# Reading the moving operand of the three-pass products in pairs of columns, and putting the columns back on the way out of PSUM

## The chip, the cores and the metric

The kernel runs on one core of one Trainium2 chip. The metric is the device time of one execution in microseconds (us); for the kernel before, three runs gave a median of 481.45 us, from 481.04 to 482.91 us.

## What is computed

The reference is a linear-attention recurrence whose output, laid out by token, goes through a two-matrix feed-forward block with a smooth gate:

```
for t in range(S):                                  # S = 768, batch 4, 8 heads, head size 48
    cur = einsum('bhd,bhe->bhde', u * k[t], v[t])
    y[:, :, t] = einsum('bhd,bhde->bhe', r[t], state + cur)
    state = w * state + einsum('bhd,bhe->bhde', k[t], v[t])
x = y as 3072 tokens x 384
h = x @ w_in                                        # 384 x 2048
g = h * tanh(softplus(h))
out = g @ w_out                                     # 2048 x 384
```

All inputs and the output are float32.

## The kernel before

**Groups and tiles.** The 768 time steps are cut into 6 groups (`NC`) of 128 steps; a group has 4 attention steps (one per batch row, `B`), and so 512 tokens (`T`). For each group the feed-forward block runs over 16 tiles of 128 hidden features (`NF`), two of which make a batch (`FB`). An up tile multiplies 3 slices of `w_in` (`KT`) with the group's x into one PSUM bank `hp` of 128 x 512; there are two such banks, used in turn. A copy, on VectorE (DVE) or ScalarE (ACT), takes `hp` to `hb` in SBUF (`evacuate`, L1214). ACT then runs Sigmoid, Arctan and Sin over the batch of two tiles (L1025 to L1031), DVE multiplies (L1041), and the result is split into a high part `gh` (L1045) and a rest `gl` (L1049). A down tile multiplies `gh` and `gl` with slices of `w_out` and adds into three PSUM banks `acc0` to `acc2`, which stay open over all 16 tiles of a group; then `put` (L1069) copies them out and sends them to memory.

**Three-pass products.** From the second group on, every product is made of three matmuls in the type float32r (four bytes an element): high weight by high operand, high weight by rest, rest of the weight by high operand. In `matmul(out, lhsT, rhs)` the `lhsT` is the stationary operand (the weights, 128 x 128) and `rhs` the moving one (128 x 512):

```
for n, (a, m) in enumerate(((wh, mh), (wh, ml), (wl, mh))):
    matmul(out, lhsT=a, rhs=m, start=first and n == 0, stop=last and n == 2, skip_group_check=skip)
```

`up` (L1013) calls it for `hp`, with x read as four runs of 128 elements, 256 apart; `down` (L1053) calls it for `acc`, with 512 elements in a row; so does `down_last` (L1320) for the last batch, written out by pass. In the first group, the up tiles 8 to 15 (`FROM`) are three-pass products on `xp` (`up_unit`, L1098), with 512 elements in a row; the down tiles 14 and 15 (`FROM2`) are three-pass products in `down_unit` (L1131). All other products of the first group are plain float32 ones, which the machine runs as two passes each, on weights left in their raw words (`wraw`, every second 32-bit word of the raw block is used). The trace names float32r as f32.

**Order.** The program is written out in full, with an order per engine that a planner works out (`Flow`): each piece of work names what it waits for and its cost on an engine, and the planner runs a list schedule. `tile_cost` (L1078) gives the costs of up and down tiles, `dve` and `act` those of the copies. The order of TensorE is mostly: up tiles of the next batch, down tiles of an earlier one, with the attention steps between. Loads go out on SP, stores mostly on ACT's queue. `matmul` at L355 is the helper that issues every matmul, so all of TensorE has this one line and the tiles tell them apart.

Of the kernel before, what the change touches and what calls it, by code (L numbers as in the profile page):

```python
# [28 lines left out]
KT = DM // 128  # L29
NF = DFF // 128  # L30
# [21 lines left out]
T = B * C  # L52
# [17 lines left out]
UNITS = [(h, c) for h in range(2) for c in range(AHEAD)] + [(None, f) for f in range(WG * AHEAD, NF)]  # L70
# [24 lines left out]
FROM, FROM2 = 8, 14  # L95
# [129 lines left out]
def dve(cols, fast=False):  # L225
    return {"dve": 0.06 + cols / (1900 if fast else 950)}


def act(cols):
    return {"act": 0.1 + cols / 1060}  # L230


class Us(float):
    n = 0
# [10 lines left out]
def pe(us, n):  # L245
    us = Us(us)
    us.n = n
    return {"pe": us}
# [3 lines left out]
def rwkv_mish_kernel(ctx, tc, rkT, rkN, vN, wT, w_in, w_out, consts, rkF, vF, wF, uF, outT):  # L252
    nc = tc.nc
# [99 lines left out]
    def matmul(out, lhsT, rhs, **flags):  # L353
        nonlocal count
        ins = nc.tensor.matmul(out, lhsT=lhsT, rhs=rhs, **flags)  # L355
        first, count = count, count + (4 if lhsT.dtype == F32 else 2)
        k = (count - 1 - BLOCK0 % BLOCK) // BLOCK
        if k != (first - 1 - BLOCK0 % BLOCK) // BLOCK:
            crossed[k] = ins
        return ins  # L360
# [95 lines left out]
    def convert(c):  # L456


        v = nc.vector
        yield f"raw{c}"  # L460
        yield f"issued{c}"
        if c >= 2:
            yield f"whole{c - 2}"
        raw = raws[c]
        up, low = raw[:, :, 1], raw[:, :, 0]
        r = low.bitcast(F32)
        yield act(WE)
        nc.scalar.activation(r, low, AF.Copy, bias=2.0, scale=2.0**-51)
        yield dve(WE, True)
        e = stage.tile([128, WE], F32, name="we", tag="we", bufs=2)  # L470
        eu = e.bitcast(U32)
        v.tensor_scalar(out=eu, in0=up, scalar1=3, scalar2=None, op0=ALU.logical_shift_left)
        yield dve(WE)
        v.scalar_tensor_tensor(out=eu, in0=up, scalar=0x80000000, in1=eu, op0=ALU.bitwise_and, op1=ALU.bitwise_xor)
        yield dve(WE)
        v.tensor_tensor(out=up.bitcast(I32), in0=e.bitcast(I32), in1=r.bitcast(I32), op=ALU.add)  # L476
        whole[W_ORDER[c]] = up.bitcast(F32)
        flow.set(f"whole{c}")
        flow.set("e%d,%d" % W_ORDER[c])
# [501 lines left out]
    def hp_tile(event=None):  # L981
        hp_log.append(event)
        return halves[len(hp_log) % 2]
# [12 lines left out]
    def three(out, wh, wl, mh, ml, first, last, skip=False):  # L996
        for n, (a, m) in enumerate(((wh, mh), (wh, ml), (wl, mh))):
            matmul(out, lhsT=a, rhs=m, start=first and n == 0, stop=last and n == 2, skip_group_check=skip)
# [14 lines left out]
    def up(o, j, event=None):  # L1013
        f, T = o.f + j, o.T
        hp = hp_tile(event)
        for k in range(KT):
            fs = slice((k * WG + f % WG) * 128, (k * WG + f % WG + 1) * 128)
            w = parts[0, f // WG]
            three(hp[:, :T], w[:, 0, fs], w[:, 1, fs], o.x[:, k, :, 0], o.x[:, k, :, 1], k == 0, k == KT - 1)
        return hp[:, :T]  # L1020


# [27 lines left out]

    accs = {}

    def down(o, j):  # L1053
        f = o.f + j
        for mt in range(KT):
            if f == 0:
                accs[mt] = ps.tile([128, 512], F32, name=f"acc{mt}", tag=f"acc{mt}")
            ws = slice(f % WG * DM + mt * 128, f % WG * DM + (mt + 1) * 128)
            a = accs[mt][:, : o.T]
            w = parts[1, f // WG]  # L1060
            three(a, w[:, 0, ws], w[:, 1, ws], o.gh[:, j], o.gl[:, j], f == 0, f == NF - 1)

    def out_buffer(mt):

        if mt < 2:
            return stage.tile([128, 512], F32, name="ob", tag="ob")
        return stage.tile([128, WE], F32, name="we", tag="we", bufs=2)

    def put(engine, mt, T, *cols, queue=nc.scalar):  # L1069
        ob = out_buffer(mt)  # L1070
        (nc.scalar.copy if engine == "act" else nc.vector.tensor_copy)(out=ob[:, :T], in_=accs[mt][:, :T])  # L1071
        n = T // len(cols)
        for k, at in enumerate(cols):
            queue.dma_start(outT[mt * 128 : (mt + 1) * 128, at], ob[:, k * n : (k + 1) * n])
# [23 lines left out]
    def up_unit(n):  # L1098
        h, c = UNITS[n]
        if n >= BY_STEP:  # L1100
            flow.fill = None
        hp = hp_tile(f"h{n}")
        if n < BY_STEP:
            return hp
        if h is None and c >= FROM:
            w, xp = parts[0, c // WG], x_parts[0]
            for k in range(KT):
                fs = slice((k * WG + c % WG) * 128, (k * WG + c % WG + 1) * 128)
                three(hp, w[:, 0, fs], w[:, 1, fs], xp[:, 0, k], xp[:, 1, k], k == 0, k == KT - 1)
            return hp  # L1110
        for i in range(1 if h is None else WG):
            f = c if h is None else c * WG + i
            at, steps = (slice(0, T), slice(0, B)) if h is None else (slice(i * HT, (i + 1) * HT), slice(2 * h, 2 * h + 2))
            for k in range(KT):
                fs = slice((k * WG + f % WG) * 128, (k * WG + f % WG + 1) * 128)
                matmul(
                    hp[:, at], lhsT=whole[0, f // WG][:, fs], rhs=xs[0][:, k, steps, 0], start=k == 0, stop=k == KT - 1
                )
        return hp
# [93 lines left out]

    def evacuate(n, o, j, h):  # L1214
        engine = yield {**dve(o.T), **act(o.T)}
        (nc.scalar.copy if engine == "act" else nc.vector.tensor_copy)(out=o.hb[:, j], in_=h)  # L1216
        flow.set(f"h{n}")

    def second(b):
# [100 lines left out]
    def down_last(b):  # L1320

        o, w = batches[b], parts[1, NW - 1]
        n = FB * b + o.n - 1

        def products(mt, j, low):
            f = o.f + j
            ws = slice(f % WG * DM + mt * 128, f % WG * DM + (mt + 1) * 128)
            for k in range(1 if low else 2):
                matmul(
                    accs[mt][:, :T], lhsT=w[:, k, ws], rhs=(o.gl if low else o.gh)[:, j], start=False,  # L1330
                    stop=low and f == NF - 1,
                )

        yield "w1,%d" % (NW - 1)
        for j in range(o.n):
            yield f"high{b},{j}"
            yield pe(0.92, 8)
            for mt in range(2):
                products(mt, j, False)
        yield f"gated{b}"  # L1340
        for mt in range(KT):
            yield pe(0.46 if mt < 2 else 1.4, 4 if mt < 2 else 12)
            for low in (True,) if mt < 2 else (False, True):
                for j in range(o.n):
                    products(mt, j, low)
            flow.start(output(NC - 1, mt), n - L_PUT)

    def output(g, mt):
        engine = yield {**dve(T), **act(T)} if g < NC - 1 else act(T)
        last = g == NC - 1 and mt < KT - 1  # L1350
        put(engine, mt, T, slice(g * T, g * T + T), queue=nc.sync if last else nc.scalar)
        flow.set(f"put{g},{mt}")


# [32 lines left out]
    for c in range(len(W_ORDER)):  # L1387
        i, f = W_ORDER[c]
# [16 lines left out]
    with tc.If(in_range < 128 * N_FLAGS):  # L1405
# [48 lines left out]
        with tc.tile_pool(name="any2", bufs=1) as work:  # L1454
            raws = [work.tile([128, WE, 2], U32, name=f"raw{i}") for i in range(2)]
            ws = [work.tile([128, 2, WE], F32R, name=f"ws{i}") for i in range(2)]
# [8 lines left out]
            o = Batch()  # L1465
# [5 lines left out]
            with tc.For_i(0, S, 128) as t0:  # L1471
                for b in range(B):
# [4 lines left out]
                    for k in range(KT):  # L1477
                        nc.tensor.transpose(
                            out=yt[:, k * 128 : (k + 1) * 128], in_=xt[:, k].rearrange("t q e -> t (q e)"), identity=unit32
                        )  # L1480
                    t = yt[:, : KT * 128].rearrange("m (k t) -> m k t", k=KT)
# [4 lines left out]
                with tc.For_i(0, NW, 1) as f:  # L1486
                    for raw, source, w in zip(raws, (w_in, w_out), ws):
# [8 lines left out]
                            out=eu, in0=top, scalar=0x80000000, in1=eu, op0=ALU.bitwise_and, op1=ALU.bitwise_xor  # L1496
                        )
                        nc.vector.tensor_tensor(
                            out=top.bitcast(I32), in0=e.bitcast(I32), in1=bottom.bitcast(I32), op=ALU.add
# [3 lines left out]
                            out=w[:, 1], in0=top.bitcast(F32), in1=w[:, 0].bitcast(F32), op=ALU.subtract  # L1503
                        )
                    for j in range(WG):
                        hp = hp_tile()
                        for k in range(KT):
                            fs = slice((k * WG + j) * 128, (k * WG + j + 1) * 128)
                            xh, xl = (x[:, k, i].rearrange("m b t -> m (b t)") for i in range(2))
# [8 lines left out]
                    for j in range(WG):  # L1518
                        for mt in range(KT):
                            fs = slice(j * DM + mt * 128, j * DM + (mt + 1) * 128)  # L1520
                            three(accs[mt], ws[1][:, 0, fs], ws[1][:, 1, fs], o.gh[:, j], o.gl[:, j], False, True, True)
                for mt in range(KT):
                    at = [bass.ds(t0 * B + (2 * c + b // 2) * C + b % 2 * CK, CK) for b in range(B) for c in range(2)]
                    put("act", mt, o.T, *at)
# [69 lines left out]
```

## Time and profile before

| | |
|---|---|
| median of 3 runs | 481.45 us (481.04 to 482.91) |
| the profiled execution, its own time | 480.58 us |
| its span, first to last instruction | 478.8 us |
| mean granted clock of TensorE | 0.999 |
| TensorE busy | 471.0 us, 98% |
| weight loads busy (beside matmuls) | 382.8 us, 80% |
| VectorE busy | 372.1 us, 78% |
| ScalarE busy | 385.6 us, 81% |
| mean memory traffic | 126 GB/s |

PE is TensorE's matmuls, PEld its weight loads, DVE is VectorE, ACT is ScalarE. A matmul's own duration is longer than its distance from the next one, since matmuls are pipelined: where eighteen of them run in a row, the distance between the first starts of two such rows divided by 18 is what one costs.

### The profile page before, as it was taken

The page shows a single profiled execution, that of the slowest core. Times are in us where ns is not written, and L with a number is a line of the kernel's source. Part 1 is how long each engine was busy: PE and PEld are TensorE (multiplying, and loading weights), DVE is VectorE, ACT ScalarE, POOL GpSimd, SP SyncE. Part 2 cuts the span into 40 slices and gives each one's busy share as a digit, 9 for nine tenths or more (in the row PEclk, how much of TensorE's full clock was granted, in tenths as well). Part 3 has the DMA queues.
Part 4 walks back from the last instruction along what each step waited for, and adds up shares of the span by engine and source line. Part 5 has one row for each costly group of instructions (what it writes and reads, how often), then busy time and mean ns, then how long its engine had stood idle before and what let it go on. Part 6 is the DMA issues. An engine that isn't in the chain of part 4 may idle for free.

```text
span 478.8 us, 11517 instructions
## 1 busy us (share of the span) xinstructions
PE 471.0 (98%) x4918; PEld 382.8 (80%) x4918; DVE 372.1 (78%) x594; ACT 385.6 (81%) x505; POOL 5.1 (1%) x31
## 2 busy tenths in 40 slices
PE   8999999999999999999999999999999999999996
PEld 5788988757888888888888888888887888888884
DVE  6899999987998895879776799965788655556551
ACT  5669999997899875886677978788967797979971
POOL 1000000000000000000000000000000000000000
PEclk9999999999999999999999999999999999999999
DMA  8766685330421330336042464421454132212001
GB/s 314 286 215 234 226 305 196 127 117 1 155 84 45 101 94 22 109 108 231 21 164 67 166 204 157 172 70 64 166 174 142 35 114 66 67 66 66 2 0 70
DMA packets 20168, 60.14 MB, mean 126 GB/s; under 512 B 3312, under 2 KB 4304, under 8 KB 20112
## 3 DMA queue, kind: packets, MB, share of 16 engines
q1 hardware_dynamic: 17664, 55.11, 34.1%
q10 hardware_dynamic: 2448, 4.25, 2.4%
q8 instruction: 39, 0.64, 0.5%
q14 instruction: 17, 0.14, 0.1%
HBM read 52.57 MB, written 4.72 MB: 120 GB/s over the span
## 4 chain that ended last, share of the span: by engine, by line
PE 97%; DVE 1%; DMA 1%; issue 0%; POOL 0%; ACT 0%; SPq 0%; POOLq 0%
PE hp L355 45%; PE acc L355 43%; PE pa L355 5%; PE yt L355 3%; DMA rk<-in_rkT_dram 1%; PE pb L355 1%; PE idle L355 1%; POOL stamp L795 0%; DVE wraw L476 0%; DVE P L725 0%; DVE x L945 0%; DVE q L605 0%; ACT we L1071 0%; DVE S L884 0%; DVE S L879 0%
## 5 line engine op out<-in xcount | busy, mean ns | idle before, releaser
L355 PE MATMUL hp<-x,w 128*128 128x512 f32 x720 | 173.0, 392 | 0.0
L355 PE MATMUL acc<-gh,w 128*128 128x512 f32 x492 | 157.9, 390 | 0.0
L355 PEld LDWEIGHTS hp<-x,w 128*128 128x128 f32 x720 | 134.2, 188 | 28.6 <-issue 0.5
L355 PEld LDWEIGHTS acc<-gh,w 128*128 128x128 f32 x492 | 92.4, 188 | 19.4
L355 PE MATMUL acc<-gl,w 128*128 128x512 f32 x246 | 95.1, 389 | 0.0
L1025 ACT ACT_TABLE_LOAD x47 | 60.3, 1283 | 15.0 <-DVE hb L1041 13.1
L1041 DVE TENSOR_TENSOR hb<-hb,fa 128x1024 f32<-128x1024 f32 x40 | 48.8, 1220 | 28.4 <-ACT fa L1031 28.3
L1216 DVE COPY hb<-hp 128x512 f32<-128x512 f32 x58 | 39.9, 688 | 37.7 <-PE hp L355 37.2
L1031 ACT ACT_TABLE_LOAD x47 | 60.3, 1283 | 1.3 <-DVE ob L1071 0.5
L1025 ACT ACTIVATE fa<-hb,small 128x1024 f32<-128x1024 f32 x48 | 55.4, 1153 | 5.9 <-DVE hb L1041 5.1
L355 PEld LDWEIGHTS acc<-gl,w 128*128 128x128 f32 x246 | 46.2, 188 | 9.5
L1028 ACT ACTIVATE fa<-fa 128x1024 f32<-128x1024 f32 x48 | 50.9, 1060 | 0.7
L1031 ACT ACTIVATE fa<-fa 128x1024 f32<-128x1024 f32 x47 | 49.8, 1060 | 0.5
L1049 DVE TENSOR_TENSOR gl<-hb,gh 128x1024 fp32r<-128x1024 f32 x40 | 48.7, 1219 | 1.1 <-ACT gh L1045 0.7
L1216 ACT COPY hb<-hp 128x512 f32<-128x512 f32 x38 | 22.0, 581 | 25.2 <-PE hp L355 25.2
L355 PE MATMUL acc<-gf,wraw 128*128 128x256 f32 (+1 forms) x132 | 37.7, 438 | 0.8 <-PE hp L355 0.8
L355 PEld LDWEIGHTS acc<-gf,wraw 128*128 128x128 f32 x132 | 25.8, 196 | 10.3 <-issue 6.8
L1045 DVE CAST gh<-hb 128x1024 fp32r<-128x1024 f32 x34 | 23.4, 689 | 5.1 <-PE acc L355 4.1
L601 DVE TENSOR_TENSOR rk<-rk,TR 112x1024 f32<-112x1024 f32 x22 | 26.8, 1218 | 0.6 <-DMA rk<-in_rkT_dram 0.6
L355 PE MATMUL hp<-x,wraw 128*128 128x256 f32 x96 | 22.4, 386 | 0.0
L355 PEld LDWEIGHTS hp<-x,wraw 128*128 128x128 f32 x96 | 18.4, 196 | 2.0
L355 PE MATMUL hp<-xp,w 128*128 128x512 f32 x72 | 19.0, 411 | 0.0
(147 smaller groups left out, 542.6 us busy)
## 6 DMA issues: line engine op xcount, KB each, us to landing
wraw<-in_w_in_dram SPq DMA_DIRECT2D x16, 768.0 KB, 4.8
wraw<-in_w_out_dram SPq DMA_DIRECT2D x16, 768.0 KB, 4.6
rk<-in_rkT_dram SPq DMA_DIRECT2D x22, 512.0 KB, 4.1
rkn<-in_rkN_dram SPq DMA_DIRECT2D x18, 384.0 KB, 4.6
v<-in_vN_dram SPq DMA_DIRECT2D x22, 256.0 KB, 4.6
out_dram<-ob ACTq DMA_DIRECT2D x10, 256.0 KB, 2.1
x<-x SPq DMA_DIRECT2D x60, 32.0 KB, 2.0
out_dram<-we ACTq DMA_DIRECT2D x6, 256.0 KB, 2.6
```

The source lines that it names most:

```text
L355: ins = nc.tensor.matmul(out, lhsT=lhsT, rhs=rhs, **flags)
L601: nc.vector.tensor_tensor(out=ab, in0=ab, in1=TR[:112].unsqueeze(1).broadcast_to([112, 4, NP, CK]), op=ALU.mult)
L1025: nc.scalar.activation(o.g, o.hb, AF.Sigmoid, bias=bias_ln2, scale=1.0)
L1028: nc.scalar.activation(o.g, o.g, AF.Arctan)
L1031: nc.scalar.activation(o.g, o.g, AF.Sin, scale=2.0)
L1041: nc.vector.tensor_tensor(out=o.hb, in0=o.hb, in1=o.g, op=ALU.mult)
L1045: (nc.scalar.copy if engine == "act" else nc.vector.tensor_copy)(out=o.gh, in_=o.hb)
L1049: nc.vector.tensor_tensor(out=o.gl, in0=o.hb, in1=o.gh.bitcast(F32), op=ALU.subtract)
L1216: (nc.scalar.copy if engine == "act" else nc.vector.tensor_copy)(out=o.hb[:, j], in_=h)
```

## The change

The moving operand of the three-pass products is read in another order: column 0, column 256, column 1, column 257, and so on (`woven`, for `down`, `down_last` and the first group's `xp` products), or, in `up`, element 0 of run 0, element 0 of run 1, element 1 of run 0, and so on through runs 0 and 1, and then the same for runs 2 and 3 (the runs are 256 elements apart). The matmul's output is written in the order in which the columns come, so the columns of `hp` and, from the second group on, of `acc` are permuted. The copies `evacuate` and `put` read PSUM with a step of two elements (8 bytes) and so write `hb` and the output buffer in the old order. The three-pass down tiles 14 and 15 of the first group, in `down_unit`, stay as they were. The planner's costs stay too.

```diff
--- before.py
+++ after.py
@@ -1016,7 +1016,8 @@
         for k in range(KT):
             fs = slice((k * WG + f % WG) * 128, (k * WG + f % WG + 1) * 128)
             w = parts[0, f // WG]
-            three(hp[:, :T], w[:, 0, fs], w[:, 1, fs], o.x[:, k, :, 0], o.x[:, k, :, 1], k == 0, k == KT - 1)
+            xh, xl = (o.x[:, k, :, i].rearrange("p (q a) t -> p q t a", a=2) for i in range(2))
+            three(hp[:, :T], w[:, 0, fs], w[:, 1, fs], xh, xl, k == 0, k == KT - 1)
         return hp[:, :T]
 
 
@@ -1050,15 +1051,24 @@
 
     accs = {}
 
+    def woven(a):
+
+        return a.rearrange("p (a t) -> p t a", a=2)
+
+    def unwoven(a):
+
+        return a.rearrange("p (t a) -> p a t", a=2)
+
     def down(o, j):
         f = o.f + j
+        mh, ml = woven(o.gh[:, j]), woven(o.gl[:, j])
         for mt in range(KT):
             if f == 0:
                 accs[mt] = ps.tile([128, 512], F32, name=f"acc{mt}", tag=f"acc{mt}")
             ws = slice(f % WG * DM + mt * 128, f % WG * DM + (mt + 1) * 128)
             a = accs[mt][:, : o.T]
             w = parts[1, f // WG]
-            three(a, w[:, 0, ws], w[:, 1, ws], o.gh[:, j], o.gl[:, j], f == 0, f == NF - 1)
+            three(a, w[:, 0, ws], w[:, 1, ws], mh, ml, f == 0, f == NF - 1)
 
     def out_buffer(mt):
 
@@ -1066,9 +1076,12 @@
             return stage.tile([128, 512], F32, name="ob", tag="ob")
         return stage.tile([128, WE], F32, name="we", tag="we", bufs=2)
 
-    def put(engine, mt, T, *cols, queue=nc.scalar):
+    def put(engine, mt, T, *cols, queue=nc.scalar, g=0):
         ob = out_buffer(mt)
-        (nc.scalar.copy if engine == "act" else nc.vector.tensor_copy)(out=ob[:, :T], in_=accs[mt][:, :T])
+        to, of = ob[:, :T], accs[mt][:, :T]
+        if g:
+            to, of = to.rearrange("p (a t) -> p a t", a=2), unwoven(of)
+        (nc.scalar.copy if engine == "act" else nc.vector.tensor_copy)(out=to, in_=of)
         n = T // len(cols)
         for k, at in enumerate(cols):
             queue.dma_start(outT[mt * 128 : (mt + 1) * 128, at], ob[:, k * n : (k + 1) * n])
@@ -1106,7 +1119,7 @@
             w, xp = parts[0, c // WG], x_parts[0]
             for k in range(KT):
                 fs = slice((k * WG + c % WG) * 128, (k * WG + c % WG + 1) * 128)
-                three(hp, w[:, 0, fs], w[:, 1, fs], xp[:, 0, k], xp[:, 1, k], k == 0, k == KT - 1)
+                three(hp, w[:, 0, fs], w[:, 1, fs], woven(xp[:, 0, k]), woven(xp[:, 1, k]), k == 0, k == KT - 1)
             return hp
         for i in range(1 if h is None else WG):
             f = c if h is None else c * WG + i
@@ -1213,7 +1226,13 @@
 
     def evacuate(n, o, j, h):
         engine = yield {**dve(o.T), **act(o.T)}
-        (nc.scalar.copy if engine == "act" else nc.vector.tensor_copy)(out=o.hb[:, j], in_=h)
+        to = o.hb[:, j]
+        if n >= NF:
+            h = h.rearrange("p (q t a) -> p q a t", q=2, a=2)
+            to = to.rearrange("p (q a t) -> p q a t", q=2, a=2)
+        elif UNITS[n][0] is None and UNITS[n][1] >= FROM:
+            h, to = unwoven(h), to.rearrange("p (a t) -> p a t", a=2)
+        (nc.scalar.copy if engine == "act" else nc.vector.tensor_copy)(out=to, in_=h)
         flow.set(f"h{n}")
 
     def second(b):
@@ -1327,7 +1346,7 @@
             ws = slice(f % WG * DM + mt * 128, f % WG * DM + (mt + 1) * 128)
             for k in range(1 if low else 2):
                 matmul(
-                    accs[mt][:, :T], lhsT=w[:, k, ws], rhs=(o.gl if low else o.gh)[:, j], start=False,
+                    accs[mt][:, :T], lhsT=w[:, k, ws], rhs=woven((o.gl if low else o.gh)[:, j]), start=False,
                     stop=low and f == NF - 1,
                 )
 
@@ -1348,7 +1367,7 @@
     def output(g, mt):
         engine = yield {**dve(T), **act(T)} if g < NC - 1 else act(T)
         last = g == NC - 1 and mt < KT - 1
-        put(engine, mt, T, slice(g * T, g * T + T), queue=nc.sync if last else nc.scalar)
+        put(engine, mt, T, slice(g * T, g * T + T), queue=nc.sync if last else nc.scalar, g=g)
         flow.set(f"put{g},{mt}")
 
 
```

## Rows read from the trace of the kernel before

**Rows 1.** The page, its span and busy time by engine (us, share, instructions).
```profile
span 478.8 us, 11517 instructions
...
PE 471.0 (98%) x4918; PEld 382.8 (80%) x4918; DVE 372.1 (78%) x594; ACT 385.6 (81%) x505; POOL 5.1 (1%) x31
...
PEclk9999999999999999999999999999999999999999
```

**Rows 2.** The page, the chain that ended last: shares by engine.
```profile
PE 97%; DVE 1%; DMA 1%; issue 0%; POOL 0%; ACT 0%; SPq 0%; POOLq 0%
```

**Rows 3.** Waits of PE: us in total, times, longest (first and last of five).
```profile
PE pa L355 <- DVE TR L299: 0.9, 1, 0.9
...
PE hp L355 <- POOL stamp L795: 0.4, 1, 0.4
```

**Rows 4.** The page, groups of three-pass matmuls: count | busy us, mean ns | idle before.
```profile
L355 PE MATMUL hp<-x,w 128*128 128x512 f32 x720 | 173.0, 392 | 0.0
L355 PE MATMUL acc<-gh,w 128*128 128x512 f32 x492 | 157.9, 390 | 0.0
...
L355 PE MATMUL acc<-gl,w 128*128 128x512 f32 x246 | 95.1, 389 | 0.0
...
L355 PE MATMUL hp<-xp,w 128*128 128x512 f32 x72 | 19.0, 411 | 0.0
```

**Rows 5.** The chain in order of time, three-pass products: start us, us, what.
```profile
310.89 4.08 PE acc L355 x18
314.97 4.08 PE hp L355 x18
...
457.81 16.33 PE acc L355 x72
```

**Rows 6.** The chain in order of time, plain float32 passes, 256 columns, then 512.
```profile
65.62 2.59 PE acc L355 x12
...
95.12 5.15 PE acc L355 x12
```

**Rows 7.** Timeline, two three-pass matmuls and the weight load between: start us, us.
```profile
391.98 0.39 PE L355 MATMUL acc<-gh,w 128*128 128x512 f32 x1
391.99 0.19 PEld L355 LDWEIGHTS acc<-gl,w 128*128 128x128 f32 x1
...
392.21 0.39 PE L355 MATMUL acc<-gl,w 128*128 128x512 f32 x1
```

**Rows 8.** Tile acc, weight loads, three-pass then plain: duration ns min/median/max.
```profile
L355 PEld LDWEIGHTS acc<-gl,w x246: 187/188/189, 122.2 to 473.5; 128*128 128x128 f32 x123
L355 PEld LDWEIGHTS acc<-gf,wraw x132: 193/197/198, 36.6 to 109.0; 128*128 128x128 f32 x132
```

**Rows 9.** DVE groups by form: count | busy us, mean ns | idle before, releaser.
```profile
L1041 DVE TENSOR_TENSOR hb<-hb,fa 128x1024 f32<-128x1024 f32 x40 | 48.8, 1220 | 28.4 <-ACT fa L1031 28.3
L1216 DVE COPY hb<-hp 128x512 f32<-128x512 f32 x58 | 39.9, 688 | 37.7 <-PE hp L355 37.2
...
L494 DVE TENSOR_TENSOR w<-wraw,w 128x768 fp32r<-128x768 f32 x16 | 15.2, 951 | 1.5 <-ACT w L492 1.5
```

**Rows 10.** ACT groups by form, same columns.
```profile
L1216 ACT COPY hb<-hp 128x512 f32<-128x512 f32 x38 | 22.0, 581 | 25.2 <-PE hp L355 25.2
...
L492 ACT CAST w<-wraw 128x768 fp32r<-128x768 f32 x16 | 14.3, 893 | 1.1 <-DVE wraw L476 1.0
...
L1045 ACT CAST gh<-hb 128x1024 fp32r<-128x1024 f32 x6 | 6.3, 1048 | 5.5 <-PE acc L355 3.4 <-DVE hb L1041 2.1
```

**Rows 11.** Timeline around 384 us: a copy out of hp, and hp's next use.
```profile
384.02 0.69 DVE L1216 COPY hb<-hp 128x512 f32<-128x512 f32 x1 [0.21 <-PE hp L355]
...
387.90 4.24 PE L355 MATMUL hp<-x,w 128*128 128x512 f32 x18
```

**Rows 12.** Windows: stretch, us, busy of PE, PEld, DVE, ACT, POOL, PEclk, DMA, GB/s.
```profile
105.00:180.00 75.00, 75.00 (x796) 60.16 (x795) 66.78 (x102) 65.40 (x81) 0.36 (x4) 1.00 0.25 83
...
400.00:460.00 60.00, 60.00 (x267) 49.44 (x266) 34.97 (x51) 50.94 (x52) 0.00 (x0) 1.00 0.16 53
```

## The prediction

> **What bounds the kernel now.** I read the page's busy times first: TensorE is busy for 471.0 of 478.8 us and its clock row is all nines, so it runs at its 2.4 GHz level throughout [rows 1]. A busy TensorE need not be the bound, so the chain of work that ended last comes next: 97% of it is PE [rows 2]. The waits of PE confirm it: five entries, the longest 0.9 us [rows 3]. So the kernel is one long row of matmuls, and whatever a matmul gains or loses goes into the time nearly in full, for as long as the other engines keep up. They have room, but not much: from 105 to 180 us DVE is busy for 66.78 and ACT for 65.40 of 75 us, from 400 to 460 us ACT for 50.94 of 60 [rows 12].
>
> What does a three-pass matmul cost? Not the 390 ns of the groups, which overlap, but the distance between starts. Eighteen take 4.08 us, 226.7 ns each, and 72 near the end take 16.33 us, 226.8 ns each [rows 5]. It is the same for `hp`, read in four runs, and for `acc`, read in one. Now a floor: 512 columns at one a cycle of 2.4 GHz are 213.3 ns. The plain float32 passes stand almost on such a floor: 12 passes of 256 columns take 2.59 us, 215.8 ns each, and 12 of 512 columns 5.15 us, 429 ns each [rows 6]. That is two cycles a column and 2 to 3 ns more. A three-pass matmul goes at one cycle a column and pays 226.7 - 213.3 = 13.4 ns on top, 10.9 more than a plain pass pays. These 10.9 ns are all that a better read could give back.
>
> **The change, part by part.**
>
> How many matmuls are woven: 720 on x, 72 on `xp`, and 492 + 246 = 738 into `acc` [rows 4], of which the first group's down tiles 14 and 15 (2 tiles x 3 banks x 3 passes = 18) stay. That makes 1512 woven.
>
> Where the 10.9 ns come from decides the case. The plain passes write the same banks and load weights before each pass too, but read their moving operand at half the pace and show no such surcharge [rows 6]. So I put it down to the moving read at full pace, which is the one thing that the change touches in the matmul; that the new order does away with it is a guess, since no row has TensorE reading two distant streams in turn. The bounds are wide. Best end: the distance of a plain 256-column pass, 215.8 ns, a gain of 1512 x 10.9 = 16.5 us (at the bare 213.3 ns it would be 1512 x 13.4 = 20.3). Middle: no change. Worst end: the read falls to the pace of the plain passes, two cycles a column, 429 ns [rows 6], a loss of 1512 x 202 = 306 us. The nearest rows for a step are of other engines: DVE reading every second word takes 951 ns for 768 elements, and the mean of its 512 and 1024 element rows, contiguous, is (688 + 1220) / 2 = 954: the step is free [rows 9]. ACT does the same in 893 ns against (581 + 1048) / 2 = 815, 10% more [rows 10]. Both have a step of 8 bytes, not of 1 KB, so they say that a step need not cost anything, and no more. I take the best end, because the surcharge sits with the read and these rows lie near free.
>
> The trace shows ScalarE and VectorE reading words 8 bytes apart at 0 to 10% more [rows 9, 10]. Against that speaks a rule of the Trainium skill, page "SBUF — State Buffer", section "Specifications (TRN2)": lines are 16 bytes, full bandwidth wants at least two hits on a line, and every crossing to a new one pays. By it each woven element would be a crossing, the surcharge would grow instead of going, and the sum would lie toward the worst end, at 480.58 + 306 = 787 us if the pace halves. No row here shows a read that crosses on every element.
>
> The copies. `evacuate` is woven for the 80 tiles of the groups after the first and for 8 of the first, `put` for 15 of 18: 103 copies, which now read PSUM with a step of two words. Lower bound nothing, as DVE's step in SBUF; with ACT's 10% it is 0.06 us on each ACT copy, some 2.5 us in all. Upper bound twice the cost for each element: (1220 - 688) / 512 = 1.04 ns on DVE, 0.53 us a copy, (1048 - 581) / 512 = 0.91 ns on ACT, 0.47 us a copy; some 50 us over both engines. I take nothing to 10%, the nearest rows. What hides it: a copy that begins at 384.02 us has until 387.90 for its bank, where `hp` is written next [rows 11], 3 us to spare, and the copies themselves wait for PE (37.2 us on DVE, 25.2 on ACT) [rows 9, 10]. If that cover goes, what is late next is Sigmoid on the batch, then the multiply, the split and the down tile, and PE waits there. Queued behind a copy on DVE are the splits `gl` that the down tiles read; on ACT it is the next function.
>
> Moved or added waits: none. No DMA, no instruction and no semaphore is added; PE's order is the same.
>
> What the others allow: with 16.5 us off PE, the stretch from 105 to 180 us would be some 3.5 us shorter, and DVE at 66.78 / 71.5 = 93%, ACT at 91%. The planner's order was made for the old tempo. I take off 2 us for short waits in PE there and in the first group, where 72 matmuls are woven.
>
> **Sum.** 16.5 - 2 = 14.5 us off the profiled execution's 480.58 gives 466.1; the median of the three runs stands 0.9 us above it (481.45), so the forecast is 467.0 us.
>
> **The rivals.**
>
> *The read falls to half pace (slower).* Each element of a pair becomes a fetch of its own, so a column takes two cycles, as in the plain passes. For it speaks that the full-pace read is the only one with a surcharge, so it has no slack; against it, DVE's free step [rows 9]. Price 202 ns on each of 1512, 306 us, so 787 us; it decides as soon as each column costs one cycle more. That is the direction of the rule of the page "SBUF — State Buffer" (section "Specifications (TRN2)") of the Trainium skill, which no row here bears out or refutes for TensorE. Milder forms, in which a pair costs a few per cent, cost 1512 x 2.3 = 3.4 us for each 1%. Chance 0.18.
>
> *The surcharge is not the read's (no change).* A weight load begins 0.01 us after the start of the matmul ahead of it, lasts 188 ns, and the next matmul starts some 30 ns after its end [rows 7, 8]. If that chain sets the 226.7 ns, the order of columns is indifferent. Against it: a plain pass loads for 197 ns, longer, and still comes every 215.8 ns [rows 6, 8]. Or the change simply doesn't alter what the machine does with the columns. Time 481.4 us, with the copies 480 to 483. Chance 0.15.
>
> *The copies cost twice (slightly slower).* With the read unchanged, DVE's busy time from 105 to 180 us would rise by some 5 us to 72 of 75, ACT's to 70, and PE would wait; 5 to 8 us in all, so 486 to 489 us; a matmul that is 1 to 3% slower gives the same (484 to 492). Chance 0.12.
>
> *Half of the surcharge goes.* 1512 x 5.5 = 8.3 us, 473 us. Chance 0.05.
>
> **How the numbers follow.** The forecast has 0.50. Faster by over 0.5% (2.4 us, about what a measurement of this kernel can tell from no change) are the forecast and the half gain: 0.55. The same: 0.15. Slower: the half-pace read and the dear copies or slower matmul, 0.30. The range goes from 463 us (the full gain with no waits, 481.45 - 16.5 = 465, and part of the way to the bare 213.3 ns) to 488 us, which takes in no change and most of the third case (0.10 of its 0.12); the half-pace read and the rest, 0.20, lie outside. Gain and loss both hold much: the forecast's own range is 463 to 470 us.
>
> **What would show it.** In the chain in order of time, 18 woven matmuls at 3.88 us instead of 4.08, with the 18 left plain in the first group still at 226.7 ns each; PE's share of the chain still near 97%; L1216 and L1071 within 10% of 688 and 581 ns; PE's waits up by no more than some 2 us. It is wrong if the 18 take 4.08 us or more, if the copies have doubled, or if waits of PE on `gl` or `hb` have eaten the gain.

## The result and the profile after

The changed kernel takes 467.47 us in the median of four runs (466.31 to 469.57), against 481.35 us for the kernel before on the same chip: a ratio of 0.971, 95% interval 0.967 to 0.976. The forecast was 467.0 us. The page of the changed kernel's profiled execution (its own time 468.38 us):

```profile
span 466.5 us, 11519 instructions
...
PE 456.0 (98%) x4918; PEld 384.8 (82%) x4918; DVE 374.4 (80%) x594; ACT 391.8 (84%) x505; POOL 4.5 (1%) x31
...
PEclk9999999999999999999999999999999999999999
...
PE 62%; DVE 25%; ACT 7%; issue 2%; DMA 2%; SPq 1%; ACTq 0%; DVEq 0%
```

The span is 12.3 us shorter, and PE's busy time 15.0 us shorter; the clock is the same [rows 1]. The chain is no longer 97% PE but 62%, with DVE at 25% [rows 2]: it is followed back through what released each step, and where PE waits for DVE it runs on along DVE. PE is still busy for 98% of the span. The chain in order of time of the changed kernel shows the price of a three-pass matmul (start us, us, what):

```profile
306.39 3.88 PE acc L355 x18
310.27 3.88 PE hp L355 x18
...
446.18 15.55 PE acc L355 x72
```

That is 215.6 ns each for eighteen and 216.0 for the last 72, where [rows 5] had 226.7 and 226.8. The three-pass products that were left straight, in the first group's down tiles, are a control within the same execution. The timeline of PE in the changed kernel, first three matmuls of such a tile, then three of a woven one:

```profile
122.80 0.39 PE L355 MATMUL acc<-gh,w 128*128 128x512 f32 x1
123.03 0.40 PE L355 MATMUL acc<-gl,w 128*128 128x512 f32 x1
123.26 0.62 PE L355 MATMUL acc<-gh,w 128*128 128x512 f32 x2
...
132.73 0.38 PE L355 MATMUL acc<-gh,w 128*128 128x512 f32 x1
132.95 0.38 PE L355 MATMUL acc<-gl,w 128*128 128x512 f32 x1
133.16 0.59 PE L355 MATMUL acc<-gh,w 128*128 128x512 f32 x2
```

The straight ones come 0.23 us apart (226 to 235 ns over all 18 of them, median 227), the woven ones some 0.215. The copies out of PSUM, by group (compare [rows 9, 10]):

```profile
L1235 DVE COPY hb<-hp 128x512 f32<-128x512 f32 x58 | 39.8, 686 | 14.3 <-PE hp L355 14.1
L1235 ACT COPY hb<-hp 128x512 f32<-128x512 f32 x38 | 21.9, 579 | 13.8 <-PE hp L355 13.7
```

686 and 579 ns against 688 and 581: reading PSUM in steps of two words costs nothing on either engine. The copies of `put` say the same (out of `acc` to `ob`, 688 ns on DVE and 591 on ACT, against 684 and 591). What did change is how long the copies wait for PE: 14.1 and 13.7 us against 37.2 and 25.2. The reserve of the other engines is being used up, and PE's own waits and the window from 105 to 180 us show that some of it is gone:

```profile
PE hp L355 <- DVE hb L1235: 1.6, 3, 1.0
...
PE pa L355 <- DVE rk L601: 0.6, 1, 0.6
PE hp L355 <- DVE S L884: 0.5, 1, 0.5
PE hp L355 <- DVE w L494: 0.3, 1, 0.3
```

```profile
105.00:180.00 75.00, 73.47 (x798) 61.07 (x798) 67.15 (x100) 66.77 (x81) 0.35 (x4) 1.00 0.28 89
```

None of these four waits stood in the profile before, where PE was busy for all 75 us of that stretch [rows 3, 12].

### The profile page after: what moved, and what is told of

It is laid out like the page before. It is cut to its first block, busy times and chain, and to the rows that moved or that the text cites. A ratio compares the mean times of both kernels' runs of the same rounds, so it can differ in the third digit from the quotient of the medians.

```text
span 466.5 us, 11519 instructions
## 1 busy us (share of the span) xinstructions
PE 456.0 (98%) x4918; PEld 384.8 (82%) x4918; DVE 374.4 (80%) x594; ACT 391.8 (84%) x505; POOL 4.5 (1%) x31
## 4 chain that ended last, share of the span: by engine, by line
PE 62%; DVE 25%; ACT 7%; issue 2%; DMA 2%; SPq 1%; ACTq 0%; DVEq 0%
PE acc L355 28%; PE hp L355 28%; DVE w L494 3%; PE pa L355 2%; PE yt L355 2%; DVE rk L601 2%; DVE we L474 2%; DVE wraw L476 2%; DMA rk<-in_rkT_dram 2%; DVE hb L1042 2%; DVE gl L1050 2%; DVE hb L1235 1%; ACT L1026 1%; DVE x L948 1%; DVE gf L1040 1%
## 5 line engine op out<-in xcount | busy, mean ns | idle before, releaser
L355 PE MATMUL hp<-x,w 128*128 128x512 f32 x720 | 165.2, 382 | 2.3 <-DVE hb L1235 1.6
L355 PE MATMUL acc<-gh,w 128*128 128x512 f32 x492 | 152.8, 380 | 0.0
L355 PE MATMUL acc<-gl,w 128*128 128x512 f32 x246 | 92.7, 379 | 0.0
L1042 DVE TENSOR_TENSOR hb<-hb,fa 128x1024 f32<-128x1024 f32 x40 | 48.9, 1221 | 35.7 <-ACT fa L1032 35.6
L1235 DVE COPY hb<-hp 128x512 f32<-128x512 f32 x58 | 39.8, 686 | 14.3 <-PE hp L355 14.1
L1050 DVE TENSOR_TENSOR gl<-hb,gh 128x1024 fp32r<-128x1024 f32 x40 | 48.8, 1220 | 1.4 <-ACT gh L1046 1.0
L1235 ACT COPY hb<-hp 128x512 f32<-128x512 f32 x38 | 21.9, 579 | 13.8 <-PE hp L355 13.7
L415 ACT ACTIVATE we<-wraw 128x768 f32<-128x768 f32 x16 | 19.2, 1203 | 2.7 <-DMA wraw<-in_w_out_dram 1.9
```

What stands on the lines that cost most here:

```text
L415: nc.scalar.activation(e, raw[:, :, 1].bitcast(F32), AF.Square, accum_out=to[:, 1:2])
L1042: nc.vector.tensor_tensor(out=o.hb, in0=o.hb, in1=o.g, op=ALU.mult)
L1050: nc.vector.tensor_tensor(out=o.gl, in0=o.hb, in1=o.gh.bitcast(F32), op=ALU.subtract)
```

## Experiments

### Half of the change at a time

```diff
 # up only: down and put as before
-        mh, ml = woven(o.gh[:, j]), woven(o.gl[:, j])
+        mh, ml = o.gh[:, j], o.gl[:, j]
...
 # down only: up and the xp products as before
-            xh, xl = (o.x[:, k, :, i].rearrange("p (q a) t -> p q t a", a=2) for i in range(2))
+            xh, xl = (o.x[:, k, :, i] for i in range(2))
```

> The up products and the first group's xp products stay woven (720 + 72 matmuls), the down products and put are as before. Theory: the surcharge of 10.9 ns sits in the moving read of each matmul by itself, so it goes matmul by matmul: 18 matmuls of hp in 3.88 us, 18 of acc in 4.08 us, 792 x 10.9 = 8.6 us off, a ratio of 0.98 to the kernel before. Rival (the surcharge is one of the weight load chain or of a stream that must be all of one kind): acc and hp stand at one common value between, or acc falls too.

> The counterpart: down products and put woven (720 matmuls), up and xp products as before. Theory: acc 3.88 us for 18, hp 4.08 us, 720 x 10.9 = 7.8 us off, a ratio of 0.984; together with the up-only kernel's gain it should make the whole 14 to 16 us. Rival (what helps is in the copies out of hp, or only the read of x in runs is slow): no gain here, ratio 1.0.

Measured: 474.6 us for up only (ratio 0.985, 0.980 to 0.991) and 474.0 us for down only (0.984, 0.978 to 0.989). Gains of 6.6 and 7.2 us against the 481.23 us of the kernel before on that chip make 13.8 us, as the whole change does. The chain in order of time, up only, then down only:

```profile
303.83 3.88 PE hp L355 x18
307.72 4.13 PE acc L355 x18
```

```profile
303.91 4.10 PE hp L355 x18
308.01 3.88 PE acc L355 x18
```

Each kind of product has its own price by the order of its own read: the theory holds, and the rival of a common cause falls. Neither half is worth quite its sum (8.6 and 7.8 us). In these kernels the straight rows stand at 4.10 to 4.13 us in places, so part of the difference can be straight matmuls of more than 226.7 ns; how large a part isn't shown.

### How far apart, and how many streams

```diff
+    TABLE = {1: 2, 2: 4, 3: 16, 4: 64, 5: 128}       # group: distance of a pair
+    def ordered(a, g):
+        return a.rearrange("p (q a t) -> p q t a", a=2, t=TABLE[g])
...
+    TABLE = {1: 4, 2: 8, 3: -2, 4: -4, 5: -16}       # the other kernel: streams, or minus the step
+        return a.rearrange("p (a t) -> p t a", a=n) if n > 0 else a.rearrange("p (t a) -> p a t", a=-n)
```

> Up as before (4.08 us for 18 throughout). In down the pairs are 2, 4, 16, 64 and 128 elements apart in groups 1 to 5 (8, 16, 64, 256 and 512 bytes). Theory (two neighbours in the read order must come from different 16-byte pieces to be fetched side by side): 2 apart stays at 226.7 ns, 4 and more give 215.8. Rival 1 (distant banks are needed, such as 1 KB): all of these stay at 226.7 or only the widest gain. Rival 2 (any order other than straight on will do): 2 apart gains as well. By the Trainium skill's rule on lines (page 'SBUF — State Buffer') crossings cost, so 4 and more would be slower than 226.7.

> Up as before. In down, groups 1 to 5 read: four streams 128 apart, eight streams 64 apart, every 2nd element (two sweeps), every 4th (four sweeps), every 16th. Theory (a new 16-byte piece for each word is no burden, and a run of words in one piece is): all but every 2nd are at 215.8 ns, every 2nd at 215.8 or 226.7. Rival (two streams are kept open, more are not): four and eight streams, and every 4th and 16th, which never return to a piece at once, fall to about 429 ns, the pace of the plain passes.

Each kernel ran once (474.3 and 623.5 us); what counts here is the price of a matmul within each group. The chain in order of time, distances of 2, 4, 16, 64 and 128 elements, one row of each group:

```profile
142.47 4.08 PE acc L355 x18
...
206.00 3.88 PE acc L355 x18
...
308.58 3.88 PE acc L355 x18
...
379.73 3.88 PE acc L355 x18
...
435.87 3.88 PE acc L355 x18
```

The same for four streams, eight streams, every 2nd, every 4th and every 16th element:

```profile
153.78 5.07 PE acc L355 x18
...
266.87 8.85 PE acc L355 x18
...
351.72 8.30 PE acc L355 x18
...
463.64 8.28 PE acc L355 x18
...
561.86 7.80 PE acc L355 x18
```

A pair 2 elements apart, that is within 16 bytes, gains nothing; 4 elements (16 bytes) and any more give the whole gain: so far as forecast. The second kernel refutes the other half of the theory. Four streams cost 282 ns a matmul, eight 492, and steps of 2, 4 and 16 cost 433 to 461, about the two cycles a column of the plain passes (429 ns, [rows 6]). So among these orders the gain is bound to just two streams, to which the read returns at once. The rival's picture, two places kept open and no more, has the direction right for four and eight streams and for steps of 4 and 16, but four streams are far from the 429 ns that it named; for steps of 2, which take two words of each 16 bytes in a row, it does not say why they are as slow. The rule of the Trainium skill (page "SBUF — State Buffer", section "Specifications (TRN2)") that every crossing to a new 16-byte line pays agrees with the steps of 4 and 16 and with eight streams. It does not hold for two streams, which cross on every element and are the fastest order; and steps of 2, which hit each line twice and so cross half as often as steps of 4, cost the same (461 against 460 ns).

### The surcharge by itself

```diff
+    def row(m, rhs, still=False):
+        for i in range(24):
+            lhsT = w[:, i % 2, :1].broadcast_to([128, m]) if still else w[:, i % 2, :m]
+            matmul(yt[:m, : math.prod(rhs.shape[1:])], lhsT=lhsT, rhs=rhs, start=True, stop=True)
+    for m, n in ((128, 512), (128, 384), (128, 256), (64, 512), (32, 512)):
+        row(m, gh[:, :n])
+        row(m, woven(gh[:, :n]))
...
```

> The changed kernel with thirteen rows of 24 float32r matmuls behind its last product, written to a bank that nobody reads: 512, 384 and 256 columns on 128 weight columns, then 512 on 64 and on 32, each straight and in pairs; then 512 columns from one repeated word; then 512 straight and in pairs with the weights read from one repeated word. The other engines are nearly idle there, so contention with them is out. Theory (the straight read loses a share of its pace): the surcharge of 10.9 ns falls with the columns, 8.2 at 384 and 5.5 at 256, does not depend on the weights, and is there without other engines. Rival 1 (a fixed cost for each matmul): 10.9 ns at every length. Rival 2 (the weight load takes turns with the moving read): half at 64 weight columns, a quarter at 32, and none with the repeated weight word. Rival 3 (the chain of weight load and matmul sets the distance): 512, 384 and 256 columns all stay near 226 ns straight.

The timeline of PE behind the last product; each line is one row of the bench (start, from the first start to the last end, tile and shape, count), straight then in pairs at 512, 384 and 256 columns, then straight on 64 and on 32 weight columns:

```profile
461.61 5.15 PE L355 MATMUL yt<-gh,w 128*128 128x512 f32 x22
467.04 4.91 PE L355 MATMUL yt<-gh,w 128*128 128x512 f32 x22
472.18 4.00 PE L355 MATMUL yt<-gh,w 128*128 128x384 f32 x22
476.36 3.90 PE L355 MATMUL yt<-gh,w 128*128 128x384 f32 x23
480.33 2.80 PE L355 MATMUL yt<-gh,w 128*128 128x256 f32 x22
483.19 2.51 PE L355 MATMUL yt<-gh,w 128*128 128x256 f32 x21
485.88 5.45 PE L355 MATMUL yt<-gh,w 128*64 128x512 f32 x23
...
496.58 5.49 PE L355 MATMUL yt<-gh,w 128*32 128x512 f32 x23
```

The time of a line runs to the end of its last matmul. Less that one's own duration (0.39 us straight and 0.38 in pairs at 512 columns, 0.34 and 0.33 at 384, 0.28 at 256) and divided by the count less one, these are 227 and 216 ns, 174 and 162, 120 and 112, and then 230 and 232. Above the floor of columns / 2.4 GHz (213.3, 160 and 106.7 ns) a straight matmul on 128 weight columns stands 13 to 14 ns at every length, a paired one 2.5 at 512 and 384 columns and 5 at 256. The 112 ns at 256 columns may not be the price of the read: 128 columns take 112 ns too, in either order (the second bench, below), so something else holds both there. The theory that I had written down, a share of the pace, is refuted: it wanted the surcharge to halve at 256 columns. It is nearly a fixed cost of each straight matmul, the first rival, though not one figure: on 64 and 32 weight columns it is 17 and 19 ns. The second falls as well: with half or a quarter of the weight columns, and with the weights read from one repeated word (232 ns straight, 216 in pairs), the surcharge is not smaller but a little larger. So does the third, since a matmul of 256 columns comes every 120 ns behind a full weight load. A moving operand that repeats one word took 219 ns, so a read without any alternation can shed more than half of the surcharge too. Behind the first row, beside which ACT still made one copy (0.55 us), DVE and ACT did nothing, so contention with them isn't the cause either.

> The changed kernel with twelve rows of 24 float32r matmuls behind its last product, into a bank that nobody reads: 512 columns straight and in pairs by turns; 448, 320 and 128 columns, each straight, then in pairs; 512 backwards; 512 in pairs 4 apart; 512 in two streams 256 apart taken two words at a time, then four words at a time; 512 straight. Theory (a fixed 13 ns for every straight matmul, 2.5 for one in pairs, charged to the matmul itself): by turns the distances alternate between 227 and 216; 448 takes 200 straight and 189 in pairs, 320 takes 146 and 136; pairs 4 apart 216; backwards 227. Rival 1 (it is charged to the change from one straight matmul to the next, so that a matmul in pairs ahead of it covers it): by turns all at 216. Rival 2 (a share of the pace, 2.1%): 198 against 189 at 448 columns, 141 against 136 at 320. For the two streams taken by more than one word: if only words that alternate between pieces help, two and four words at a time are at 227.

The timeline again: by turns straight and in pairs at 512; 448 straight, in pairs; 320 straight, in pairs; pairs 4 apart; two streams taken two words at a time, four words at a time:

```profile
460.54 5.29 PE L355 MATMUL yt<-gh,w 128*128 128x512 f32 x23
465.87 4.62 PE L355 MATMUL yt<-gh,w 128*128 128x448 f32 x22
470.72 4.33 PE L355 MATMUL yt<-gh,w 128*128 128x448 f32 x22
475.22 3.38 PE L355 MATMUL yt<-gh,w 128*128 128x320 f32 x22
478.73 3.15 PE L355 MATMUL yt<-gh,w 128*128 128x320 f32 x22
...
493.03 4.91 PE L355 MATMUL yt<-gh,w 128*128 128x512 f32 x22
498.00 8.16 PE L355 MATMUL yt<-gh,w 128*128 128x512 f32 x24
505.99 5.92 PE L355 MATMUL yt<-gh,w 128*128 128x512 f32 x23
```

By turns the mean is 223 ns, and the starts alternate: 231 or 232 ns behind a straight one, 215 or 216 behind one in pairs. So a matmul pays for its own order, and one in pairs ahead of it doesn't cover it. At 448 and 320 columns the straight ones take 203 and 146 ns, 16 and 13 above the floor, those in pairs 189 and 136, both 2.5 above: nearly fixed once more, and no share of the pace, which wanted 198 and 141. Pairs 4 apart take 216 ns. Two words at a time cost 333 ns and four 250, worse than straight, where I had expected 227; of the two-stream orders tried only the strict alternation helps. Backwards settled at 233 to 234 ns, and 128 columns took 112 in either order.

### What could be better still

```diff
 # the planner's cost of a three-pass tile
-        return pe(9 * (T + 33) / 2400, 18) if g else pe(3 * 4 * (T + 3) / 2400, 24 if halved else 12)
+        return pe(9 * (T + 6) / 2400, 18) if g else pe(3 * 4 * (T + 3) / 2400, 24 if halved else 12)
...
 # pairs of the down products 4 elements apart
+        return a.rearrange("p (q a t) -> p q t a", a=2, t=4)
```

> The changed kernel with the planner told of the new cost of a three-pass tile (9 x 518 cycles in place of 9 x 545), so that its order is made for the new tempo. Theory (some 2 us of the gain went into waits of PE that an order for the new tempo avoids): 465 to 466 us, a ratio of 0.967. Rival (the hand-tuned shifts fit the old order only): the same or slower, 467 to 472.

> The changed kernel again, on the same chip as the two beside it: 467 us, a ratio of 0.971.

> The changed kernel with the pairs of the down products 4 elements apart (neighbouring 16-byte pieces) instead of 256; up as changed. Theory: 215.8 ns as before, the same time as the changed kernel within 0.3%; ScalarE's and VectorE's reads of every second word (L415, L492, L494), which grew from 893 to about 1200 ns where 256-apart pairs ran beside them, go back to about 900 where a down product runs beside them, which is off the chain. Rival (those slow reads did cost PE time): 1 to 3 us faster.

Measured on one chip, against 480.86 us before: 470.42 us with the new costs (ratio 0.978, 0.977 to 0.980), 467.16 us for the changed kernel again (0.972, 0.970 to 0.974), 467.05 us with near pairs (0.972, 0.969 to 0.975). The rival was right on the time: an order made afresh for the true tempo, with the shifts left as they were (`SHIFT` in the kernel), is 3.3 us worse than the old one. That the shifts fit the old order only is the likely reason, but no run varies them, so it isn't shown. The profiled execution is the slowest of the five (474.14 us); its granted clock falls twice after 15 us (0.77 from 15 to 30 us, 0.96 from 140 to 180), where that of the changed kernel beside it stays at 1.00, so what the order alone costs can't be read from it. Its longest wait of PE is in the attention steps of the beginning:

```profile
PE pb L355 <- DVE kn L679: 1.8, 1, 1.8
```

Near pairs make no difference to the time. No version tried beats the changed kernel.

## Why the prediction was right

*The size of the gain for each matmul.* The floor taken from the plain passes was the right one: the woven matmul stands at 215.6 to 216 ns, where the prediction had 215.8, and 1512 of them make the 16.5 us of the sum.

*Where the surcharge sits.* It was put down to the moving read. The control tiles, the two halves and the bench bear it out: the order of the read alone switches it on and off, on the same weights and the same bank. That this new order would do away with it was a guess that no row could carry, and there the prediction had luck: it leaned on the steps of DVE and ACT, which lie near free (and were read by setting copies out of PSUM beside two-input work in SBUF), while a step of two words costs TensorE 461 ns a matmul, and two neighbouring choices, four streams and pairs 2 apart, would have lost time or gained nothing. One idea in the prediction has to be corrected. The plain passes have no surcharge, and I read that as the pace of the read, which I had from their distances alone; the bench shows that the surcharge isn't a share of the pace but 13 to 19 ns for each straight matmul and 2.5 for each paired one, down to 320 columns. With 512 columns throughout, the sum could not tell the two apart.

*The rivals.* The half-pace read was real, at 433 to 492 ns, but it belongs to steps and to eight streams, not to two. "The surcharge is not the read's" falls by the bench. The copies, bounded from nothing to twice the price, came out at nothing (686 and 579 ns).

*The waits.* I took 2 us off for them. From 1512 x 10.9 = 16.5 us the medians keep 13.9, so 2.6 us went. In the two profiled executions the span fell by 12.3 us and PE's busy time by 15.0: PE's idle time grew by 2.7 us, from 7.8 to 10.5. Of its new waits, 1.5 us fall between 105 and 180 us, where it was busy throughout: 0.7 on copies out of `hp`, 0.6 on an attention step's `rk`, 0.3 on a split of the weights, all on DVE, in the stretch that the prediction named. Another 0.5 us (at 209 us, on the attention state) and 1.0 us (at 283 us, on a copy out of `hp`) come later, where it named none. Why PE's busy time fell by 15.0 us and not by 16.5 is not shown. One sign that the prediction named failed: PE's share of the chain did not stay near 97%, it fell to 62%.

## What to carry to other kernels

Measure what a matmul costs by the distance between starts, set against the columns over the clock and against a row of another type in the same trace: a constant remainder on every matmul is worth looking for when a thousand of them stand on the chain. On this chip a float32r moving operand read as two alternating streams 16 to 1024 bytes apart costs 11 ns less for each matmul of 512 columns than the same operand read straight, and putting the columns back in the copy out of PSUM is free; four streams, or steps of 2, 4 or 16, are much slower, so such an order has to be timed by itself. An order of work made for one tempo can be better at the new tempo than one planned afresh (467.2 against 470.4 us here).

## What the runs showed beyond that

The paired read takes something from other engines that the straight one leaves them. ACT's and DVE's reads of every second word of the raw weights became slower: the rows of three lines of the kernel before, then of the changed one (duration ns min/median/max):

```profile
L492 ACT CAST w<-wraw x16: 863/889/931, 54.5 to 152.0; 128x768 fp32r<-128x768 f32 x16
L494 DVE TENSOR_TENSOR w<-wraw,w x16: 944/950/959, 56.5 to 153.8; 128x768 fp32r<-128x768 f32 x16
L415 ACT ACTIVATE we<-wraw x16: 872/896/916, 238.2 to 437.5; 128x768 f32<-128x768 f32 x16
```

```profile
L492 ACT CAST w<-wraw x16: 880/902/1244, 55.4 to 153.2; 128x768 fp32r<-128x768 f32 x16
L494 DVE TENSOR_TENSOR w<-wraw,w x16: 948/1086/1226, 57.4 to 154.8; 128x768 fp32r<-128x768 f32 x16
L415 ACT ACTIVATE we<-wraw x16: 1111/1204/1245, 236.5 to 427.6; 128x768 f32<-128x768 f32 x16
```

Contiguous work beside it, such as the multiply at 1221 ns against 1220, is not touched. The slowing depends on the distance of the pairs. In the kernel with the distances by group, L415 in the groups with 4, 16 and 64 elements:

```profile
L415 ACT ACTIVATE we<-wraw x3: 871/882/911, 237.4 to 267.1; 128x768 f32<-128x768 f32 x3
...
L415 ACT ACTIVATE we<-wraw x5: 896/902/931, 296.3 to 345.3; 128x768 f32<-128x768 f32 x5
...
L415 ACT ACTIVATE we<-wraw x5: 910/1181/1227, 358.8 to 406.6; 128x768 f32<-128x768 f32 x5
```

With near pairs in the down products beside 256-apart ones in the up products, its median was 1018 ns (872 to 1249), and the trace tells which are slow: the eight that run mostly beside up products take 1113 to 1249 ns, the seven beside down products 872 to 922, and the one beside an attention step 917. In the kernels with half of the change, too, it is the woven half that slows L415. So it is the distant pairs beside them that slow these reads. L415 is not among the lines that the page names on the chain, but L494 is, at 3%, and PE waits 0.3 us for it. Near pairs in the down products left the time as it was, but beside the up products L494 stayed slow there (up to 1199 ns); what those reads cost is therefore not shown. Why two streams shed the fixed cost of a matmul, why four and a step of two words do not, and what the distant pairs hold that the stepped reads need, stays open.
